# Four key units of linear attention projected at later tiles of the feed-forward, in a fused attention and feed-forward kernel

## The chip, the cores and the metric

The kernel runs on one core of a Trainium2 chip. The metric is the device time of one execution in microseconds (us).

## What is computed

A linear attention over 8 batches of 8 heads, 576 tokens and 64 channels, with 128 projected features that are taken with both signs, and then a feed-forward network on its output (4608 tokens, 512 to 2048 to 512 channels) with the Mish function in the middle. All in float32.

```
def phi(x):
    proj = np.einsum('bhsd,df->bhsf', x, w_phi)
    proj = proj - np.max(np.abs(proj), axis=-1, keepdims=True)
    return np.concatenate([np.exp(proj), np.exp(-proj)], axis=-1)
q_p, k_p = (phi(q), phi(k))
kv = np.einsum('bhsf,bhsd->bhfd', k_p, v)
z = np.sum(k_p, axis=2)
num = np.einsum('bhsf,bhfd->bhsd', q_p, kv)
den = np.einsum('bhsf,bhf->bhs', q_p, z)[..., None] + 1e-06
x = num / den            # heads side by side: 4608 x 512
h = x @ w_in
sp = np.where(h > 20.0, h, np.log1p(np.exp(np.minimum(h, 20.0))))
g = h * np.tanh(sp)
out = g @ w_out
```

## The kernel before

**Work on the keys.** Two heads make a pair, the 32 pairs of all batches lie behind each other, and their 18432 rows are cut into 36 key units of 512 rows, 0 to 35. A unit has five steps. `k_load` fetches its 256 KB; `v_load` fetches the values of the pairs that begin in it (two `v` buffers); `k_proj` multiplies by `w_phi` into two PSUM banks, and DVE takes the maximum of the absolute values (L174) and subtracts it (L175) into two `e` tiles, of which there are six; `k_exp` makes the two exponentials of each tile on ACT (L216, L217), two calls per unit; `k_sum` multiplies with the values into an open sum `kvps` of the pair, which a DVE copy (L233) ends. A pair has 576 rows, so its sum stays open from one unit to the next and keeps one of the four banks of the pool `ps_att`. That pool also serves the projections, the transposes `dt`, the numerators `num` and the sums of the weights' low parts.

**Work on the queries.** The tokens are cut into 18 chunks of 256, each in two groups of heads. `q_proj` projects (for chunks after the first, one of its two banks is from the pool `ps_h`, which has two and serves the feed-forward too), `q_turn` transposes and makes the exponentials (L251, L253), `q_num` multiplies with the sums, `q_out` transposes the result (L278). The numerator of (2, 0), chunk 2 and group 0, needs the sums up to pair 5, and (2, 1) needs those up to pair 7, which ends with key unit 8.

**The feed-forward.** For a chunk it has 16 tiles of 128 hidden channels. `ff_in` makes one tile (twelve matmuls, L300), after every second one `mish` follows (L308, a table of ACT other than that of the exponential), which is split in a high and a low part (L312 on ACT, L313 on DVE), and `ff_out` (L330) follows some four tiles later. Chunks 0 and 1 are worked on in halves: tiles 0 to 7 are the first half of chunk 0, 8 to 15 the first half of chunk 1, 16 to 23 and 24 to 31 the second halves. The partial sums of the first halves are copied away by ACT (L335). Both weights are split into parts in the kernel as well: `split_weight` uses ACT (L118, L119, L131), DVE (L121 to L125) and POOL (L127, L135, L136), 32 times, from tile -13.2 to tile 20.1. Its word tiles share three buffers with the tiles `u` of Mish.

**The order.** Each step is an event with a time, in units of feed-forward tiles, and the program calls the steps in the order of these times (L349 to L397). TensorE works in that order exactly. The other engines' queues are ordered by a planner, which goes by its own costs; only the activations with a table keep the program's order among them (`table`, L151). `FIRST_STEPS` (L35 to L37) lists the first steps by hand, as (time, key unit, query). From tile 14 on a loop adds one key unit and one query group every eight tiles: at 14 key unit 9 with query (2, 0), at 22 key unit 10 with query (2, 1).

A step at time t without a query and after tile 1 sets its other times from its own alone: the loads at t - 4 (`v_load` at t), the projection at t - 0.04, the exponentials at t + 1.2 and t + 1.7, the sum at t + 3.77:

```
if not first and not query:
    exps, tsum = (t + 1.2, t + 1.7), t + 3.8
```

Of the kernel before, what the change touches and what calls it, by code (L numbers as in the profile page):

```python
# [32 lines left out]
NK, LEAD = B * NHP * S // 512, 5  # L33

FIRST_STEPS = ((-14.0, 0, None), (-12.5, 1, None), (-11.0, 2, None), (-9.5, 3, None), (-8.0, 4, None), (-6.6, None, 0),  # L35
               (-5.2, None, 1), (-2.0, None, 2), (1.0, None, 3), (5.0, 5, None), (7.0, 6, None), (9.0, 7, None),
               (11.0, 8, None))  # L37

FE0, FE1, FSUM, FX, FLAST = 0.9, 1.2, 2.1, 3.1, 1.0
E0, E1, GX = 0.27, 0.36, 0.6  # L40
# [389 lines left out]
```

## Time and profile before

| | us |
|---|---|
| median of three runs | 1200.73 |
| lowest and highest of them | 1200.13, 1201.69 |
| the profiled execution | 1200.22 |
| its span, first to last instruction | 1198.40 |
| TensorE busy (matmul) | 1143.7 |
| ACT busy | 639.0 |
| DVE busy | 471.7 |
| POOL busy | 97.6 |

A row of the timeline gives the start, the duration, engine, line, operation, the output and the inputs, and the count of instructions merged in it. In square brackets stands how long the engine was idle just before, and what ended that.

### The profile page before, as it was taken

What the parts mean: (1) busy time and instruction counts of PE and PEld (TensorE: products, weight loads), DVE (VectorE), ACT (ScalarE), POOL (GpSimd) and SP (SyncE); (2) the same over time, 40 slices, a digit from 0 to 9 for tenths busy, and PEclk for the clock granted to TensorE, in tenths of its full rate; (3) what the DMA queues carried; (4) which work ended last, traced back from release to release, by engine and by line L of the source; (5) the groups of instructions that cost most, each with busy time, mean ns of one, the idle gap of its engine ahead of it and who ended that gap; (6) DMA issues with size and microseconds to landing.
All of it is one profiled execution on the core that took longest, in us unless ns stands there. A gap on an engine that the chain in (4) does not pass through costs nothing.

```text
span 1198.4 us, 26666 instructions
## 1 busy us (share of the span) xinstructions
PE 1143.7 (95%) x11696; PEld 1018.5 (85%) x11696; DVE 471.7 (39%) x977; ACT 639.0 (53%) x1051; POOL 97.6 (8%) x86
## 2 busy tenths in 40 slices
PE   6788877999999999999999999999999999999998
PEld 5666766999898989898989898998989898998997
DVE  4655888443333333333333333333333332222311
ACT  6867756555555555555554545454545455555422
POOL 2233667000000000000000000000000000000000
PEclk9899888999999999999999999999999999999999
DMA  9901110111111111101111111001111100000000
GB/s 349 354 27 30 59 29 19 48 48 29 40 31 48 29 38 30 35 25 45 31 48 30 48 31 39 28 30 48 30 48 31 47 19 28 1 19 19 1 19 18
DMA packets 25028, 57.68 MB, mean 48 GB/s; under 512 B 2768, under 2 KB 2896, under 8 KB 24912
## 3 DMA queue, kind: packets, MB, share of 16 engines
q1 hardware_dynamic: 24912, 55.98, 13.8%
q8 instruction: 92, 1.51, 0.5%
q14 instruction: 24, 0.20, 0.1%
HBM read 46.53 MB, written 9.44 MB: 47 GB/s over the span
## 4 chain that ended last, share of the span: by engine, by line
PE 81%; ACT 8%; DVE 4%; DMA 2%; issue 2%; POOL 1%; SPq 0%; ACTq 0%; POOLq 0%; DVEq 0%
PE h L300 32%; PE o L330 29%; PE num L184 6%; PE kvps L184 6%; PE pp_q L169 3%; PE pp_k L169 2%; PE dt L251 2%; DMA words_out<-w_out 2%; ACT L253 1%; ACT e_q L253 1%; PE xt L278 1%; ACT gh L312 1%; ACT e_k L216 1%; ACT e_k L217 1%; DMA kraw<-qT 1%
## 5 line engine op out<-in xcount | busy, mean ns | idle before, releaser
L300 PE MATMUL h<-xTh,win 128*128 128x256 f32 x2304 | 463.9, 285 | 12.2 <-DVE e_q L175 8.0
L300 PEld LDWEIGHTS h<-xTh,win 128*128 128x128 f32 x2304 | 375.8, 190 | 26.5 <-issue 8.4
L330 PE MATMUL o<-wout,gh 128*128 128x512 f32 x1152 | 370.7, 403 | 9.6 <-ACT part L335 5.6
L313 DVE TENSOR_TENSOR gl<-u,gh 128x256 fp32r<-128x256 f32 x288 | 125.9, 456 | 570.3 <-ACT gh L312 562.7
L300 PE MATMUL h<-xTl,win 128*128 128x256 f32 x1152 | 325.9, 283 | 0.0
L330 PEld LDWEIGHTS o<-wout,gh 128*128 128x128 f32 x1152 | 197.8, 189 | 42.9 <-ACT osb L343 9.2
L330 PE MATMUL o<-wout,gl 128*128 128x512 f32 x576 | 228.2, 396 | 0.0
L300 PEld LDWEIGHTS h<-xTl,win 128*128 128x128 f32 x1152 | 218.9, 190 | 8.4
L308 ACT ACTIVATE u<-h 128x512 f32<-128x512 f32 x144 | 86.1, 598 | 173.1 <-PE h L300 165.8
L281 ACT CAST xTh<-xt 128x512 fp32r<-128x512 f32 x36 | 21.2, 589 | 287.7 <-PE xt L278 287.2
L330 PEld LDWEIGHTS o<-wout,gl 128*128 128x128 f32 x576 | 108.7, 189 | 26.6
L312 ACT CAST gh<-u 128x256 fp32r<-128x256 f32 x288 | 110.6, 408 | 18.7 <-PE o L330 6.4
L184 PE MATMUL kvps<-v,e_k 128*64 128x66 f32 x2560 | 88.2, 229 | 6.6 <-ACT e_k L217 6.6
L308 ACT ACT_TABLE_LOAD x73 | 93.7, 1283 | 1.3
L184 PEld LDWEIGHTS kvps<-v,e_k 128*64 128x64 f32 x2560 | 82.5, 143 | 13.7 <-ACT e_k L217 7.5
L253 ACT ACTIVATE e_q<-dt 128x512 f32<-128x512 f32 x144 | 77.9, 596 | 14.4 <-PE dt L251 14.1
L253 ACT ACT_TABLE_LOAD x64 | 82.1, 1283 | 1.0
L184 PE MATMUL num<-kv,e_q 128*64 128x66 f32 x2304 | 74.8, 222 | 1.7 <-DVE e_k L175 1.3
L184 PEld LDWEIGHTS num<-kv,e_q 128*64 128x64 f32 x2304 | 70.9, 137 | 5.4 <-issue 4.6
L169 PEld LDWEIGHTS pp_k<-w_phi,kraw 64*128 64x128 f32 x576 | 38.8, 199 | 25.2 <-issue 21.4
L169 PE MATMUL pp_k<-w_phi,kraw 64*128 64x128 f32 x576 | 46.7, 299 | 12.8 <-issue 5.4
L174 DVE TENSOR_REDUCE m_k<-pp_k 128x4 f32<-128x512 f32 x72 | 46.5, 685 | 22.6 <-PE pp_k L169 22.6
(70 smaller groups left out, 851.4 us busy)
## 6 DMA issues: line engine op xcount, KB each, us to landing
v<-va SPq DMA_DIRECT2D x32, 330.0 KB, 3.4
kraw<-kT SPq DMA_DIRECT2D x36, 256.0 KB, 2.7
out<-osb SPq DMA_DIRECT2D x36, 256.0 KB, 2.0
qraw<-qT SPq DMA_DIRECT2D x35, 256.0 KB, 2.6
words_in<-w_in SPq DMA_DIRECT2D x16, 512.0 KB, 8.7
words_out<-w_out SPq DMA_DIRECT2D x16, 512.0 KB, 8.7
kraw<-qT SPq DMA_DIRECT2D x1, 256.0 KB, 8.6
w_phi<-w_phi SPq DMA_DIRECT2D x1, 64.0 KB, 1.8
```

Source lines behind the costliest of these rows:

```text
L169: nc.tensor.matmul(ps[j][:, n], raw[rows, n * P:(n + 1) * P], w_phi2[rows], start=True, stop=True)
L174: nc.vector.tensor_reduce(m, ps[j], axis=AX.X, op=ALU.max, apply_absolute_value=True)
L184: nc.tensor.matmul(ps[rows], lhsT[:, rows], rhs[h], start=start, stop=stop, skip_group_check=True)
L216: table(nc.scalar.activation(e[:, 1, :], e[:, 0, :], AF.Exp))
L251: nc.tensor.transpose(ps[:, n * P:(n + 1) * P], e[:, 0, n * P:(n + 1) * P], ident)
L253: table(nc.scalar.activation(e[:, s, :], ps, AF.Exp, scale=2.0 * s - 1.0))
L281: nc.scalar.copy(hi, ps)
L300: nc.tensor.matmul(ps, w[:, wcol], x[:, cc % 2, :], start=(n == 0), stop=(n == 11))
L308: table(nc.scalar.activation(u, hv, AF.Mish))
L312: nc.scalar.copy(gh, u[:, f * CH:(f + 1) * CH])
L313: nc.vector.tensor_sub(gl, u[:, f * CH:(f + 1) * CH], gh.bitcast(F32))
L330: nc.tensor.matmul(ps, g[:, cols], w, start=(i == first and k == 0), stop=(i == end and k == 2))
```

## The change

Four times in `FIRST_STEPS` are other ones. Key units 5, 6, 7 and 8 have 5, 7, 9 and 11 before, and 6, 9, 12 and 16 after.

```
 FIRST_STEPS = ((-14.0, 0, None), (-12.5, 1, None), (-11.0, 2, None), (-9.5, 3, None), (-8.0, 4, None), (-6.6, None, 0),
-               (-5.2, None, 1), (-2.0, None, 2), (1.0, None, 3), (5.0, 5, None), (7.0, 6, None), (9.0, 7, None),
-               (11.0, 8, None))
+               (-5.2, None, 1), (-2.0, None, 2), (1.0, None, 3), (6.0, 5, None), (9.0, 6, None), (12.0, 7, None),
+               (16.0, 8, None))
```

All steps of these units move with it, by 1, 2, 3 and 5 tiles. Unit 8 is now projected at 15.96 and summed at 19.77, so its projection comes after that of unit 9 and query (2, 0) at tile 14, and its sum still before that of unit 9 at 21.97. The raw keys of unit 8 are asked for at 12 instead of 7, after those of unit 9 and query (2, 0) at 10. The values of pair 8, asked for at 14, come in the program ahead of the sum of unit 7, which moves from 12.77 to 15.77.

## Rows read from the trace of the kernel before

**Rows 1.** Busy time by stretch, columns in its first line: around the change, and the rest.

```profile
core 0: us, PE busy (x) PEld busy (x) DVE busy (x) ACT busy (x) POOL busy (x), PEclk, DMA share, GB/s
115.00:190.00 75.00, 57.32 (x577) 49.64 (x574) 57.65 (x80) 52.58 (x81) 49.47 (x37) 0.86 0.13 41
260.00:1190.00 930.00, 925.67 (x9405) 834.67 (x9404) 308.81 (x697) 465.54 (x766) 0.00 (x0) 1.00 0.10 31
```

**Rows 2.** TensorE's waits, 90 to 215 us: us in total, times, longest.

```profile
PE h L300 <- DVE e_q L175: 8.0, 1, 8.0
PE o L330 <- ACT part L335: 5.6, 2, 2.9
PE h L300 <- POOL win L136: 4.1, 2, 3.7
PE pp_k L169 <- ACT wout L147: 2.5, 1, 2.5
```

**Rows 3.** Timeline of TensorE, the five places A to E.

```profile
120.28 1.42 PE L169 MATMUL pp_k<-w_phi,kraw 64*128 64x128 f32 x14 [2.50 <-ACT wout L147]
...
141.22 1.00 PE L330 MATMUL o<-wout,gh 128*128 128x512 f32 x2 [2.88 <-ACT part L335]
...
159.85 0.55 PE L300 MATMUL h<-xTh,win 128*128 128x256 f32 x1 [8.04 <-DVE e_q L175]
...
187.20 0.79 PE L300 MATMUL h<-xTh,win 128*128 128x256 f32 x2 [3.72 <-POOL win L136]
...
193.22 1.22 PE L330 MATMUL o<-wout,gh 128*128 128x512 f32 x2 [2.73 <-ACT part L335]
```

**Rows 4.** Busy time by stretch, columns as in the first group: behind place C.

```profile
159.00:165.00 6.00, 5.15 (x18) 4.38 (x18) 5.80 (x10) 4.44 (x7) 4.05 (x5) 0.50 0.00 0
```

**Rows 5.** The chain that ended last, in order of time: start, us, what.

```profile
105.92 0.63 ACT e_k L216
...
144.39 0.63 ACT e_k L216
...
147.22 0.68 ACT w_out L118
...
159.10 0.61 DVE e_q L175
```

**Rows 6.** Timeline of TensorE, and groups by line and shape.

```profile
149.15 1.16 PE L169 MATMUL pp_k<-w_phi,kraw 64*128 64x128 f32 x16
165.23 2.15 PE L184 MATMUL kvps<-v,e_k 128*64 128x66 f32 x64
L174 DVE TENSOR_REDUCE m_k<-pp_k 128x4 f32<-128x512 f32 x72 | 46.5, 685 | 22.6 <-PE pp_k L169 22.6
L175 DVE TENSOR_TENSOR e_k<-pp_k,m_k 128x512 f32<-128x512 f32 x72 | 46.7, 681 | 0.0
L216 ACT ACTIVATE e_k<-e_k 128x512 f32<-128x512 f32 x72 | 45.4, 631 | 0.0
```

**Rows 7.** Timeline of DVE, key unit 8 and a weight.

```profile
137.06 1.27 DVE L174 TENSOR_REDUCE m_k<-pp_k 128x4 f32<-128x512 f32 x2
138.25 0.41 DVE L125 TENSOR_SCALAR t_in<-w_in 128x512 uint32<-128x512 uint32 x1
```

**Rows 8.** Timelines of ACT and DVE between C and D.

```profile
169.12 0.62 ACT L131 CAST win<-w_in 128x512 fp32r<-128x512 f32 x1 [4.25 <-POOL t_in L127]
...
180.54 0.60 ACT L308 ACTIVATE u<-h 128x512 f32<-128x512 f32 x1
...
183.33 0.62 ACT L131 CAST win<-w_in 128x512 fp32r<-128x512 f32 x1 [0.87 <-POOL t_in L127]
183.97 1.28 ACT L118 ACT_TABLE_LOAD   x1
...
187.18 0.68 ACT L118 ACTIVATE w_out<-words_out 128x512 f32<-128x512 f32 x1 [0.79 <-POOL win L136]
170.37 1.50 DVE L125 TENSOR_SCALAR t_in<-w_in 128x512 uint32<-128x512 uint32 x1 [2.46 <-POOL wout L136]
```

## The prediction

> **What bounds the kernel now.** I read the page's slices first, then the busy time by stretch. TensorE is the bound after 260 us: there it is busy for 925.67 of 930 us, so nothing there can be won by moving four projections [rows 1]. The first 260 us hold its idle time, and the change lies in 95 to 200 us of them. Between 115 and 190 us TensorE has 57.32 busy us of 75; no other engine fills that stretch either: ACT 52.58, DVE 57.65, POOL 49.47. So this stage is bound by a chain that hops between engines, each of which works through its own queue in order.
>
> The view of TensorE's waits between 90 and 215 us says where that chain ends: the four largest causes come to 20.2 us [rows 2]. I place them by the timeline. A: 2.50 us at 120.28, the projection of key unit 7, for a buffer of `ps_att`. B: 2.88 us at 141.22. C: 8.04 us at 159.85, ff_in of tile 14, which needs the `h` bank that q_proj(2, 0) took and DVE has not read out. D: 3.72 us at 187.20 and the rest of 4.1 behind it, ff_in of tile 20, for the POOL half of splitting the weights `in_*_3`. E: 2.73 us at 193.22 [rows 3]. After the gap C the granted clock stands at 0.50, the lower of the two levels (1.2 of 2.4 GHz), from 159 to 165 us [rows 4]. A gap thus costs more than its length.
>
> The chain of waits, in order of time, shows what C hangs on: from 105.92 us until C ends it runs over ACT, POOL and DVE, and not over TensorE. Key units stand in it by name: an exponential of unit 5 at 105.92, one of unit 8 at 144.39, and, right before C ends, the DVE work of query (2, 0) at 159.10, behind that of unit 9 [rows 5]. A and B don't stand in that chain: taking A or B alone away would only lengthen C. So what counts is how much ACT and DVE have to do ahead of 159.85, and then ahead of 187.
>
> **The change, part by part.** No instruction is added or removed. One key unit is 16 matmuls of 64x128 in a burst of 1.16 us, 64 or 80 sum matmuls (2.15 us in the row at 165.23, where it is 64), two maxima and two subtractions on DVE (2 x 685 + 2 x 681 ns = 2.73 us) and four exponentials on ACT (two pairs of L216 and L217, which write the same shape, so 4 x 631 ns = 2.52 us) [rows 6]. In the chain's rows they count less, since they overlap: two maxima take 1.27 us together, and L125 of a weight, which the chain waits for, starts 1.19 us behind the first of them [rows 7].
>
> ACT first. Mish activations follow each other every second tile, and the exponentials of a unit fall between two of them. Before: unit 5 behind the Mish of tile 5, unit 6 behind 7, unit 7 behind 9, unit 8 behind 11, none behind 13 and 17. After, from exps at t+1.2 and t+1.7: unit 5 behind 7, unit 6 behind 9, none behind 5 and 11, unit 7 behind 13, unit 8 behind 17. So two slots ahead of C (behind 5 and 11) lose their exponentials. Each slot is worth between 0.63 us (the one that stands in the chain) and 2.52 us (all four in series). I take 1.6, the middle, since in 144.39 to 147.22 other casts lie between them: 3.2 us for both.
>
> DVE ahead of C: four key units become three (unit 8 now comes after query (2, 0)). Worth from 0 to 2.73 us; I take 1.2, the delay of L125 that the rows show. Sum ahead of C: 3.2 + 1.2 = 4.4 us, bounds 0 and 7.8.
>
> Table loads: the splits' own activations (L118) pay a load of 1.28 us when they follow a Mish, as behind the Mish of tile 17, at 183.97 [rows 8]. Splits fall into slots 5, 11, 13 and 17 before and after, so I count no load saved and none added. The Trainium skill (ScalarE: Activation LUTs, Table sets: the hidden batching unit) says that cheap functions such as abs stand in every set; by that no load would be due for L118, two would be saved ahead of C and two added after it, which again leaves the sum where it is. Here the timeline does have a load in front of L118, so the row decides.
>
> What comes back after C. Unit 7's exponentials fall behind the Mish of tile 13, where ACT then waits 4.25 us for POOL (169.12): cost 0, bound 2.52 if they are queued ahead of the casts that wait ends with. Unit 8's DVE work lands behind its projection at tile 16, near 168 us, where DVE idles 2.46 us (before 170.37): I take 1.0, for what doesn't fit or pushes L125, bounds 0 and 2.73. Unit 8's exponentials fall behind the Mish of tile 17 (180.54), where ACT has 0.87 and 0.79 us idle: 2.52 - 1.66 = 0.9, bounds 0 and 2.52. TensorE gets the projection (1.16) and the sum (2.15) of unit 8 between C and D instead of ahead of C: 3.3 us, covered by the 4.1 us that it waits at D; uncovered they cost 3.3 [rows 8]. Sum after C: 1.9 us.
>
> Buffers and queues. `ps_att` has four banks, one of them held from k_sum(5) to k_sum(8) by an open `kvps`; the hold now ends at 19.77 instead of 14.77, with q_turn(2, 0) at 16.16 inside it. Its transposes come behind unit 8's two banks and two `kvps`, so the copy of `kvps_6` (L233) must be out: a wait of up to some 2 us ahead of D, under the same cover as the 3.3 us (together 5.3 against 4.1). Six `e` tiles: unit 8 takes unit 7's, free since k_sum(7) was issued just ahead. On SP the raw keys are asked for four tiles early as before. The v of batch 2's first pair (v_load(9), at 14) needs the buffer that k_sum(7) frees, now at 15.77, and SP waits for it; behind it stand only the loads at 18, and the data is wanted at 21.97, six tiles later: nothing.
>
> Sum: -4.4 + 1.9 = -2.5 us on the profiled execution. Its own time is 1200.22 us, 1.82 above its span, and 0.51 below the median of the runs shown (1200.73). The forecast is 1197.7 us.
>
> **The rivals.** What a measurement of this kernel can tell from no change is about 0.2%, here 2.4 us.
>
> (1) The weights set the time. TensorE gets through tile 20 when the split of `in_3_3` is done on POOL, behind 188 us, whatever it gained before. If the relief at slots 5 and 11 is eaten by POOL and ACT waiting for each other (L127, L131, L136), C may end earlier and D grow by as much. For it: D is a wait for POOL, and POOL's queue holds three operations for each weight. Against it: that chain begins at L118 on ACT, which starts earlier with fewer exponentials ahead. Time: 1200.2 +- 2, no change.
>
> (2) Slower: unit 8 becomes the late thing. k_sum(8) at 19.77 stands in TensorE's queue ahead of ff_in 20, and it wants exponentials that stand behind the Mish of tile 17. From the rows: 180.54 + 0.60 (Mish) + 1.28 (table) + 2.52 (exponentials) + 1.2 (two casts between, of 0.62 like the one at 183.33) = 186.2, then 2.15 of sum: tile 20 would begin at 188.4 and not only go on, as now, at 187.20. The cast of `in_3_3` at 183.33 and the copies that E waits for (L335) are pushed by up to 2.5 us each. With both, 2.5 + 2.5 = 5 us: 1205.2. It decides if unit 8's last exponential ends after 187.20 - 2.15 = 185, less what the first half of tile 20 takes. Against it: C comes earlier and carries all of this with it.
>
> (3) More is won: slots and DVE pay in full (7.8 us), and the clock stays at full level at A. Then 1192.4 us or a little less, since C's shorter gap also leaves less at half clock.
>
> **How the numbers follow.** The forecast with (3): 0.46 (its own range 1191 to 1198.3). Rival 1: 0.29. Rival 2: 0.25. For the range I take the lower bound 1191 (7.8 us and somewhat over 1 us of the half clock) and the upper 1206.5 (rival 2 and a further 1.3 for a transpose that waits uncovered: 5.3 - 4.1). This leaves some 2 in 10 outside, as the order of ACT, DVE and POOL is the planner's, and it may change more than these rows show. Faster by over 0.2%: 0.46; within: 0.29; slower: 0.25.
>
> **What would show it.** Right: no exponential of a key unit between the Mish of tile 5 and tile 7; unit 7's projection without the wait A; C's wait ends before 157 us; unit 8's DVE work in an idle stretch near 170 us; D no longer than before. Wrong: TensorE waiting at k_sum(8) for L217; the wait for POOL at tile 20 longer by what C lost; a new wait at the transposes (L251) for DVE; the same 20 us in the view of waits with other names. After 230 us nothing should differ but the offset.

## The result, and the profile after

The changed kernel is slower: 1207.62 us (median of 4 runs, 1206.69 to 1207.91) against 1200.84 for the kernel before, a ratio of 1.0049 with a 95% interval of 1.0037 to 1.0061 (the ratios in this text are those on record for the single runs; the quotient of the two medians is 1.0056, and lies in the interval). The forecast was 1197.7, in a range from 1191 to 1206.5. The profiled execution took 1207.58 us, its span is 1205.8, so 7.4 us more than before.

TensorE's waits between 90 and 215 us in the changed kernel (us in total, times, longest; it answers to [rows 2]):

```profile
PE h L300 <- ACT u L308: 9.3, 1, 9.3
PE num L184 <- DVE e_k L175: 6.0, 1, 6.0
PE kvps L184 <- ACT e_k L217: 3.6, 3, 1.7
PE pp_k L169 <- DVE e_k L175: 3.2, 1, 3.2
PE dt L251 <- DVE kv L233: 1.7, 1, 1.7
PE lo_out L144 <- ACT wout L147: 1.7, 1, 1.7
```

Of the four causes of [rows 2] the first has another releaser and the other three are gone: no wait for a bank at unit 7 (A), for POOL at tile 20 (D), or for the copies L335 (B, E). In their place stand others. A's releaser L147 is there again, at a weight's low-part sum (L144), and unit 9's projection waits 3.2 us for a bank. The largest new one is 6.0 us at the numerators `num`.

A sum of waits doesn't say which of them cost the time. For that I follow one and the same instruction in both timelines and see where the distance grows. TensorE before, then after, around tile 22 (key unit 10's projection, the second bank of the numerators, the projection of query (2, 1), the transposes of q_out(2, 0)):

```profile
198.23 1.16 PE L169 MATMUL pp_k<-w_phi,kraw 64*128 64x128 f32 x16
...
203.70 1.16 PE L184 MATMUL num<-kv,e_q 128*64 128x66 f32 x32 [1.34 <-DVE e_k L175]
204.79 1.16 PE L169 MATMUL pp_q<-w_phi,qraw 64*128 64x128 f32 x16
...
208.80 0.82 PE L278 MATMUL xt<-ident,x 128*128 128x128 f32 x4
```

```profile
198.64 1.16 PE L169 MATMUL pp_k<-w_phi,kraw 64*128 64x128 f32 x16
...
208.73 2.03 PE L184 MATMUL num<-kv,e_q 128*64 128x66 f32 x32 [5.97 <-DVE e_k L175]
210.69 2.08 PE L169 MATMUL pp_q<-w_phi,qraw 64*128 64x128 f32 x16
...
216.36 0.60 PE L278 MATMUL xt<-ident,x 128*128 128x128 f32 x4
```

Up to unit 10's projection the changed kernel is 0.41 us late. At the second numerator it is 5.03 late, since the wait there is 5.97 instead of 1.34, and at the transposes 7.56, since TensorE then works at the lower clock: the same numerators take 2.03 us instead of 1.16, the projection 2.08 instead of 1.16. The stretch behind the wait, in the changed kernel (columns as in [rows 1]), has a granted clock of 0.50, the lower level:

```profile
208.00:213.00 5.00, 4.27 (x49) 3.95 (x50) 2.82 (x9) 0.59 (x1) 3.67 (x3) 0.50 0.01 3
```

So nearly the whole loss, 7.2 of 7.4 us, lies in one place, at a step that the diff doesn't name. The second numerator needs a bank of `ps_att`; four are out (two of unit 10's projection, the open `kvps`, the first numerator), and the first to come back is the one that DVE's subtraction of unit 10 (L175) empties. DVE's timeline says why that is late. Before:

```profile
200.87 0.43 DVE L125 TENSOR_SCALAR t_out<-w_out 128x512 uint32<-128x512 uint32 x1
201.21 1.28 DVE L174 TENSOR_REDUCE m_k<-pp_k 128x4 f32<-128x512 f32 x2
202.41 0.55 DVE L121 TENSOR_SCALAR w_out<-w_out 128x512 f32<-128x512 f32 x1
202.87 1.27 DVE L175 TENSOR_TENSOR e_k<-pp_k,m_k 128x512 f32<-128x512 f32 x2
```

After:

```profile
201.79 0.43 DVE L125 TENSOR_SCALAR t_out<-w_out 128x512 uint32<-128x512 uint32 x1
202.13 0.42 DVE L121 TENSOR_SCALAR w_out<-w_out 128x512 f32<-128x512 f32 x1
202.59 1.40 DVE L122 TENSOR_SCALAR w_out<-w_out 128x512 uint32<-128x512 uint32 x1
204.02 0.69 DVE L123 SCALAR_TENSOR_TENSOR w_out<-words_out,w_out 128x512 uint32<-128x512 uint32 x1
204.63 1.48 DVE L313 TENSOR_TENSOR gl<-u,gh 128x256 fp32r<-128x256 f32 x1
206.04 0.41 DVE L125 TENSOR_SCALAR t_out<-w_out 128x512 uint32<-128x512 uint32 x1
206.38 0.41 DVE L313 TENSOR_TENSOR gl<-u,gh 128x256 fp32r<-128x256 f32 x1
206.71 1.28 DVE L174 TENSOR_REDUCE m_k<-pp_k 128x4 f32<-128x512 f32 x2
```

Both queues come to the end of weight 30 (L125) within 0.92 us of each other. Before, unit 10's maxima are next. After, the four steps of weight 31 and the low part of the Mish of tile 21 have been put ahead of them, 4.6 us of work, while TensorE has had unit 10's projection ready since 199.8. DVE is 0.92 us late; the rest of the wait is other work that stands first.

### The profile page after: what moved, and what is told of

It is laid out like the page before. It is cut to its first block, busy times and chain, and to the rows that moved or that the text cites. A ratio compares the mean times of both kernels' runs of the same rounds, so it can differ in the third digit from the quotient of the medians.

```text
span 1205.8 us, 26671 instructions
## 1 busy us (share of the span) xinstructions
PE 1145.4 (95%) x11696; PEld 1020.8 (85%) x11696; DVE 470.1 (39%) x977; ACT 638.1 (53%) x1051; POOL 97.5 (8%) x86
## 4 chain that ended last, share of the span: by engine, by line
PE 80%; ACT 9%; DVE 4%; DMA 2%; issue 2%; POOL 1%; SPq 1%; ACTq 0%; POOLq 0%; DVEq 0%
PE h L300 31%; PE o L330 28%; PE num L184 6%; PE kvps L184 5%; PE pp_q L169 3%; PE pp_k L169 2%; PE dt L251 2%; DMA words_out<-w_out 2%; ACT L253 1%; ACT e_q L253 1%; PE xt L278 1%; ACT e_k L217 1%; ACT e_k L216 1%; ACT gh L312 1%; DMA kraw<-qT 1%
## 5 line engine op out<-in xcount | busy, mean ns | idle before, releaser
L313 DVE TENSOR_TENSOR gl<-u,gh 128x256 fp32r<-128x256 f32 x288 | 122.1, 443 | 567.1 <-ACT gh L312 559.2
L184 PE MATMUL kvps<-v,e_k 128*64 128x66 f32 x2560 | 89.3, 231 | 10.2 <-ACT e_k L217 10.1
L184 PEld LDWEIGHTS kvps<-v,e_k 128*64 128x64 f32 x2560 | 83.3, 144 | 17.2 <-ACT e_k L217 12.1
L184 PE MATMUL num<-kv,e_q 128*64 128x66 f32 x2304 | 75.6, 223 | 6.4 <-DVE e_k L175 6.0
L184 PEld LDWEIGHTS num<-kv,e_q 128*64 128x64 f32 x2304 | 71.7, 138 | 10.1 <-issue 9.4
```

Source lines behind the costliest of these rows:

```text
L184: nc.tensor.matmul(ps[rows], lhsT[:, rows], rhs[h], start=start, stop=stop, skip_group_check=True)
L313: nc.vector.tensor_sub(gl, u[:, f * CH:(f + 1) * CH], gh.bitcast(F32))
```

## The experiments

Two theories stood against each other. The DVE-order theory is the one above. The late-unit-8 theory is rival 2 of the prediction: TensorE does wait at k_sum(8) for the exponentials L217, 1.18 and 1.65 us, and this could be carried to the end (in the chain that ended last, unit 8's exponentials stand from 184.08 to 187.95 us, ahead of weight 30 on DVE):

```profile
185.89 0.45 PE L184 MATMUL kvps<-v,e_k 128*64 128x66 f32 x8 [1.18 <-ACT e_k L217]
188.00 3.35 PE L184 MATMUL kvps<-v,e_k 128*64 128x66 f32 x56 [1.65 <-ACT e_k L217]
```

Each run was timed beside the kernel before on the same chip; ratios are to that.

**1. Changed kernel, unit 10 a tile earlier.**

```
-            at(t - 0.04, k_proj, key)
+            at(t - (0.04 if key != 10 else 1.04), k_proj, key)
```

> The changed kernel, with the projection of key unit 10 one tile earlier in TensorE's order (20.96 instead of 21.96), so that DVE's queue has its maxima behind weight 30 again, as before the change, and not behind weight 31 and the Mish of tile 21. DVE-order theory: the wait of q_num(2,0) for L175 falls from 6.0 us to under 2, no half clock follows, and the time is 1200 to 1202.5. Late-unit-8 theory (TensorE's 2.8 us at k_sum(8) for L217, carried on): nothing of that is touched, the time stays at 1205 to 1208.

1201.67 us against 1201.8, ratio 0.9996 (0.9988 to 1.0005): the whole loss is gone. On DVE the maxima stand behind weight 30, and the wait is 1.64 us; the waits for L217 are as they were. TensorE and DVE in this run:

```profile
188.45 3.13 PE L184 MATMUL kvps<-v,e_k 128*64 128x66 f32 x56 [1.66 <-ACT e_k L217]
...
205.07 1.16 PE L184 MATMUL num<-kv,e_q 128*64 128x66 f32 x32 [1.64 <-DVE e_k L175]
```

```profile
202.24 0.43 DVE L125 TENSOR_SCALAR t_out<-w_out 128x512 uint32<-128x512 uint32 x1
202.58 1.28 DVE L174 TENSOR_REDUCE m_k<-pp_k 128x4 f32<-128x512 f32 x2
```

The late-unit-8 theory, which expected 1205 to 1208, falls.

**2. Changed kernel, unit 10 behind the numerators.** The same line with 0.015 instead of 1.04.

> The changed kernel, with the projection of key unit 10 behind q_num(2,0) in TensorE's order instead of ahead of it, so that the numerators find free PSUM banks; DVE's queue still has weight 31 and the Mish of tile 21 ahead of unit 10's maxima. If the wait for a bank at the numerators is the loss: that wait is gone; what TensorE now waits for is the projection's bank, for the short DVE work on the numerators, 1 to 3 us; 1201 to 1204. Late-unit-8 theory: 1205 to 1208.

1205.83 us, ratio 1.0039 (1.0025 to 1.0052), outside what I expected. The numerators wait no longer, but unit 10's projection does, 4.60 us for L268 of the numerators, which stands behind the same weight 31 and the same Mish on DVE:

```profile
207.57 1.83 PE L169 MATMUL pp_k<-w_phi,kraw 64*128 64x128 f32 x13 [4.60 <-DVE r L268]
```

So it isn't the place of the bank in TensorE's order. Whoever comes to DVE at this point waits; I had thought that short work on DVE would also be started soon.

**3. Kernel before, with DVE's order as after.** Ahead of the maxima of unit 10 (in the code, `red` is the maximum):

```
+            if name == "k_10":
+                for first in ("out_15_0", "0_6"):
+                    tc.add_manual_dep(red.ins, behind[first].name, ...)
```

(`behind` keeps the last DVE step, L125, of each weight and the last low part, L313, of each Mish.)

> The kernel before, with one thing of the changed one: on DVE the first maximum of key unit 10 is held behind the last step of weight 31 (L125) and behind the low part of the Mish of tile 21, by an order on DVE's own queue. DVE-order theory: the numerators wait 5 to 7 us instead of 1.3, with half clock behind it, and the time is 1205 to 1208. Late-unit-8 theory: unit 8 is early here, so nothing is lost but the longer wait partly: 1201 to 1203.

1207.87 us, ratio 1.0056 (1.0043 to 1.0068), with all four key units where they were before:

```profile
206.86 1.27 DVE L175 TENSOR_REDUCE m_k<-pp_k 128x4 f32<-128x512 f32 x2
...
208.73 0.67 DVE L180 TENSOR_TENSOR e_k<-pp_k,m_k 128x512 f32<-128x512 f32 x1
```

```profile
208.88 1.72 PE L189 MATMUL num<-kv,e_q 128*64 128x66 f32 x32 [4.66 <-DVE r L273]
```

The line names L273 as releaser, a short step between the two subtractions. The wait of 4.66 us is a little under the 5 to 7 expected. Not all of this run's time is the forced order's: in its profile unit 10's projection is already 1.87 us late (200.10 against 198.23; the waits for L335 and for POOL are 6.9 and 5.2 us in total there, where [rows 2] have 5.6 and 4.1). It isn't the chip, for run 4, taken on the same one, has 5.6 and 3.9. The transposes of q_out(2, 0) are 6.71 us late (215.51 against 208.80). So 6.71 - 1.87 = 4.84 of the 6.4 us by which its span of 1204.8 us is longer arise at tile 22, from the forced order.

**4. Control: kernel before, unit 10 a tile earlier.**

> The control of the first: the kernel before with the projection of key unit 10 one tile earlier. Its numerators wait only 1.3 us, so by the DVE-order theory there is at most that and a little clock to win: 1198.5 to 1201.5. If moving unit 10 is a gain by itself (then the first run would say nothing of the change): under 1197.

1200.3 us, ratio 0.9992 (0.9983 to 1.0000): as expected, and not a gain that these runs can tell from none. So the 6 us that the same edit gives back in run 1 are the change's own.

**5. The forecast's relief, taken outright.** Units 5 and 8, in the kernel before:

```
+        if n in (5, 8):
+            table(nc.scalar.activation(e[:, 0, :P], e[:, 0, :P], AF.Exp, scale=-1.0))
+            return
...
-                        halves(ps[:, j, s], es[j][:, s, i * P:(i + 1) * P], (vt...
+                        halves(ps[:, j, s], es[j][:, 0, :P] if n in (5, 8) else es[j][:, s, i * P:(i + 1) * P], (vt...
```

and for unit 8 maximum and subtraction over one block of 128 columns of four. The kernel leaves out most of these units' exponentials, so its output is not the reference's.

> The kernel before with most of what the forecast counted as relief taken away outright, to size it. Key units 5 and 8 make only one exponential of 128 columns per tile instead of two of 512, unit 8 also only a quarter of its maxima and subtractions; their sums read that slice instead, so TensorE's instructions stay and the output is not the reference's. By the forecast's steps (1.6 us for a slot with all exponentials, 1.2 us for the DVE work of a unit, here some 0.8 of each): C ends 3 us earlier, near 157, and the time falls by 3 us. If the weights set the time (rival 1): C ends earlier, the wait for POOL at tile 20 grows by the same, and the time moves by less than 1 us.

1199.27 us, ratio 0.9979 (0.9971 to 0.9988). The total, 2.5 us, is near the 3 us expected, but it doesn't come the way that was forecast: C ends at 160.19, not earlier than before, and D is longer:

```profile
160.19 0.58 PE L304 MATMUL h<-xTh,win 128*128 128x256 f32 x1 [7.16 <-ACT u L312]
...
187.91 0.79 PE L304 MATMUL h<-xTh,win 128*128 128x256 f32 x2 [4.87 <-POOL win L136]
```

What is gained comes with the copies L335, waits for which fall from 5.6 us to 2.8: E is gone, what is left is at B, and unit 10's projection starts at 196.12 instead of 198.23. With less work ahead C does not move. The Mish that it now waits for stands on ACT behind the splits' casts (L131), which wait for POOL, and waits for POOL itself:

```profile
155.43 0.62 ACT L131 CAST wout<-w_out 128x512 fp32r<-128x512 f32 x1 [3.01 <-POOL t_out L127]
156.06 1.28 ACT L312 ACT_TABLE_LOAD   x1
159.54 0.60 ACT L312 ACTIVATE u<-h 128x512 f32<-128x512 f32 x1 [2.19 <-POOL wout L136]
```

**6. Run 1, with the sum of unit 8 behind tile 20.** `at(tsum - 0.03 if key != 8 else 20.6, k_sum, key)`.

> The first experiment (changed kernel, key unit 10 projected a tile earlier), and also the sum of key unit 8 behind ff_out of tile 20 (20.6 instead of 19.77), so that TensorE doesn't wait for the exponentials L217 ahead of tile 20. If that wait of 2.8 us is what ate the forecast's gain: 1.5 to 3 us less than the first experiment, 1198.5 to 1200.5. If the split weights set when tile 20 ends anyway (rival 1): tile 20 waits for POOL instead, and the time is that of the first experiment, within 1 us.

1204.2 us, ratio 1.0020 (1.0011 to 1.0028); both expectations missed. Tile 20 does wait for POOL instead (2.26 us), and then the ff_out behind it, that of tile 16, for the copies L335 (4.18 us):

```profile
190.38 0.38 PE L300 MATMUL h<-xTh,win 128*128 128x256 f32 x1 [2.26 <-POOL win L136]
...
195.65 1.22 PE L330 MATMUL o<-wout,gh 128*128 128x512 f32 x2 [4.18 <-ACT part L335]
197.22 3.79 PE L184 MATMUL kvps<-v,e_k 128*64 128x66 f32 x64
```

The sum, now behind these gaps, runs at the lower clock (granted 0.50 from 197 to 201 us; it takes 3.79 us, where [rows 6] have 2.15). At 19.77 the sum covers the time that TensorE waits for POOL here.

**7. Unit 8 at tile 13 instead of 16.** `(6.0, 9.0, 12.0, 13.0)`.

> The changed kernel with key unit 8 at tile 13 instead of 16, units 5 to 7 as changed, nothing else. DVE's queue then has unit 10's maxima behind weight 30 and the first step of weight 31, as before the change. DVE-order theory: the numerators wait 1 to 2 us and the time is 1199.5 to 1203. If spreading units 5 to 7 were itself the loss: 1205 or more.

1202.37 us, ratio 1.0005 (0.9996 to 1.0014). The numerators don't wait at all. Units 5 to 7 in their new places, with unit 8 at 13, cost nothing that can be told.

**8. Unit 8 alone.** `(5.0, 7.0, 9.0, 16.0)`.

> Unit 8 alone moved: tiles 5, 7, 9 and 16. On DVE the maxima of unit 10 then come behind three steps of weight 31, and its subtractions behind the Mish of tile 21. DVE-order theory: the numerators wait 5 to 6 us for L175, 1205 to 1208, nearly the whole loss of the change. If the four moves share the loss: about 1202 to 1204.

1205.71 us, ratio 1.0029 (1.0018 to 1.0039). It is slow, but the wait at the numerators is 2.98 us and not 5 to 6; C is longer than before (11.13 us against the 8.04 of [rows 3]). Unit 10's projection is 2.65 us late (200.88), the transposes 5.82 (214.62): of the 5.5 us by which its span is longer, some 3.2 arise at tile 22 and the rest ahead of it.

```profile
162.47 0.55 PE L300 MATMUL h<-xTh,win 128*128 128x256 f32 x1 [11.13 <-DVE e_q L175]
...
207.98 1.16 PE L184 MATMUL num<-kv,e_q 128*64 128x66 f32 x32 [2.98 <-DVE e_k L175]
```

**9. Changed kernel, weight 31 split later.** `WTIMES[31] = 23.1`. TensorE's order stays as changed.

> The changed kernel with the split of weight 31 at 23.1 instead of 20.125, nothing else. It has no step on TensorE, so TensorE's order stays as changed. On DVE its four steps (some 2.9 us) then come behind unit 10's maxima; the Mish of tile 21 (some 1.9 us) still stands ahead of them. DVE-order theory: a part of the loss comes back, in proportion: the numerators wait 2.5 to 4.5 us instead of 6.0, and the time is 1203 to 1206. Late-unit-8 theory: no change, 1206.5 to 1208.5.

1204.24 us, ratio 1.0021 (1.0012 to 1.0030). With weight 31 out of the way and the Mish of tile 21 still ahead, the wait is 3.17 us:

```profile
207.94 1.16 PE L185 MATMUL num<-kv,e_q 128*64 128x66 f32 x32 [3.17 <-DVE e_k L176]
```

This is a dose in the middle. But not all of this run's loss is at tile 22: unit 10's projection is already 2.41 us late (200.64), the transposes 4.24 (213.04), so 1.83 of the 4.0 us by which its span is longer arise there, just what the wait has more than the 1.34 before. The ratios are thus no clean measure of the dose (2.41 us were lost elsewhere here, 2.65 in run 8, 1.87 in run 3). A cleaner one is the time from the start of k_sum(9) to the transposes of q_out(2, 0) on TensorE, which holds the numerators:

| | wait at the numerators, us | k_sum(9) to the transposes, us | ratio |
|---|---|---|---|
| run 4 | none | 7.91 | 0.9992 |
| run 7 | none | 8.39 | 1.0005 |
| kernel before | 1.34 | 9.48 | 1 |
| run 1 | 1.64 | 9.77 | 0.9996 |
| run 8 | 2.98 | 12.64 | 1.0029 |
| run 9 | 3.17 | 11.30 | 1.0021 |
| run 3 | 4.66 | 14.32 | 1.0056 |
| the change | 5.97 | 16.63 | 1.0049 |

Run 8 is out of line with run 9 because the clock falls behind its wait: the projection of query (2, 1) takes 1.83 us there and 1.16 in run 9.

**10. POOL's share of in_\*_3 taken out.** In the kernel of run 4, the four splits without L135 and L136; the low part is the rest alone:

```
+            if not (kind == "in" and j == 3):
                 nc.gpsimd.tensor_sub(wf, wf, hi.bitcast(F32))
                 nc.gpsimd.tensor_tensor(lo, wf, rest, op=ALU.add)
+            else:
+                nc.vector.tensor_copy(lo, rest)
```

> The kernel before with unit 10 projected a tile earlier (as in the fourth experiment), and the four splits of in_*_3 without POOL's last two steps: the low part is the rest alone, copied by DVE, so the output is less exact. POOL then has 8 operations of 1.3 to 1.4 us less ahead of tile 20. If the weights set when tile 20 goes on: the wait for POOL (4 us) is gone, and with the clock behind it the time falls by 3 to 7 us against the fourth experiment, 1194 to 1198. If key units and ACT's queue set it: tile 20 waits for something else, and the time moves by less than 1.5 us.

1201.99 us, ratio 1.0005 (0.9996 to 1.0013). POOL is gone from TensorE's waits, and nothing is won:

```profile
PE o L333 <- ACT part L338: 9.9, 4, 5.2
PE h L303 <- DVE e_q L178: 7.7, 1, 7.7
PE pp_k L172 <- ACT wout L150: 2.5, 1, 2.5
PE h L303 <- ACT win L131: 2.3, 1, 2.3
```

The copies L335 (here L338) wait longer on ACT, and tile 20 waits for a cast of ACT (L131). Rival 1 had tile 20 go on when POOL is done with its split; with POOL out of the way, TensorE waits for ACT's queue instead.

**11 and 12. Two tries for a faster kernel**, both on run 4: the splits of in_\*_3 earlier and those of out_8 to out_11 later (`(11.5, 14.5), (12.5, 15.5)` in WTIMES), and `NSUMMED` 18 instead of 16 (two more weights without L135 and L136 on POOL; their L121 goes from DVE to POOL, so POOL loses two operations and not the four that I counted, and the two it gets are short, 0.6 us).

> A try for a faster kernel, from the same finding: the fourth experiment with the splits of in_*_3 a tile or so earlier (12.5 to 15.5 instead of 13.5 to 17) and those of out_8 to out_11 a tile later (11.5 to 14.5). If POOL's order allows it, tile 20's wait of 4 us shrinks by 2 or 3 us: 1197 to 1200. If the buffers that splits and Mish share hold it up: 1200 to 1204.

> A second try: the fourth experiment with 18 instead of 16 weights whose low part TensorE sums, so POOL loses four operations ahead of tile 16 and TensorE gets six or so matmuls more, with two more PSUM banks passing through. If POOL's queue is what delays the later splits, the chain moves ahead by 2 to 4 us and the time falls to 1196 to 1199.5. If not, TensorE's own extra work and waits for banks show: 1200 to 1204.

1204.75 us (1.0031, 1.0019 to 1.0042) and 1201.38 us (0.9999, 0.9990 to 1.0007): neither is faster. In the first the wait for POOL is gone, but 11.1 us of waits for Mish stand there, and the waits for L335 have grown from 5.6 to 9.0; in the second TensorE waits 5.4 us for POOL. No run with the reference's whole work beats the kernel before by more than the runs can tell.

## Why the prediction was wrong, point by point

**The step that failed is the sum: it left out a term, and the relief ahead of C in it was too large.** It ran from C to D and took what follows tile 20 as given: "So what counts is how much ACT and DVE have to do ahead of 159.85, and then ahead of 187." It had no term for the numerators at tile 22. The cause was in the view of waits that I read, as `num L184 <- DVE e_k L175`, 1.34 us; I kept the four largest and dropped it. It measured 5.97, and with the clock behind it the loss is 7.16 of the 7.4 us: 4.63 of wait, and 2.53 between the second numerator and the transposes (208.80 - 203.70 = 5.10 before, 216.36 - 208.73 = 7.63 after). Run 1 takes this loss away, run 3 makes most of it in the kernel before, and run 9 gives it in part. The second failure is smaller: the relief of 4.4 us ahead of C came to 1.25, and so even with the loss at tile 22 taken away nothing is left of the 2.5 us (run 1: 0.9996, interval 0.9988 to 1.0005).

**What was said of queues.** The text went through `ps_att` at tile 16, the `e` tiles and SP, and what it found there held (the wait at the transposes L251 for the copy L233 is 1.69 us, where it had up to 2, and no wait of TensorE's ends with a load on SP). It had no wait for a bank at unit 9's projection, where 3.17 us stand, nor at the numerators. And it treated the order on DVE as that of the rows before, and said only in the range that it may change. It did change, at an instruction that the diff doesn't touch.

**Ahead of C: 4.4 us.** C ended at 158.60, 1.25 us earlier, and by a Mish on ACT instead of DVE. Unit 5's slot was empty, as said, unit 7 no longer waited at A, and the table loads came out as counted (16 between 100 and 195 us before, 16 after; in the emptied slots the load stands in front of L118, at 107.95 and 141.15). The count for the other case, that L118 needs none, was off: a slot without exponentials then saves the load for them and that for the next Mish, so four ahead of C against four behind it, and the sum stays the same. But run 5 cut the exponentials in the same two slots down to short ones, and C didn't move; the slots of 1.6 us were not in series with C. The rows that put single exponentials in the chain were true, yet without them the chain went through the neighbours: POOL's steps of the splits and the casts that wait for them. In the changed kernel:

```profile
145.50 1.83 PE L169 MATMUL pp_k<-w_phi,kraw 64*128 64x128 f32 x13 [3.17 <-DVE e_k L175]
...
158.60 0.58 PE L300 MATMUL h<-xTh,win 128*128 128x256 f32 x1 [9.34 <-ACT u L308]
```

```profile
156.02 0.62 ACT L131 CAST wout<-w_out 128x512 fp32r<-128x512 f32 x1 [2.21 <-POOL t_out L127]
156.66 1.28 ACT L308 ACT_TABLE_LOAD   x1
157.95 0.60 ACT L308 ACTIVATE u<-h 128x512 f32<-128x512 f32 x1
```

Unit 9's projection at 145.50 shows the mechanism of tile 22 once more: it waits for the subtraction of unit 7, whose maxima DVE begins at 139.04, 6.6 us after that projection's end (132.41), behind steps of weights, one of which waits 2.40 us for POOL. Here TensorE waits for C afterwards anyway; whether this delay moved C was not tried.

**After C: 1.9 us.** Unit 8's DVE work did not fall into the idle stretch near 170: its first maximum is at 178.20, 9.2 us behind the start of the projection (168.96), between the steps of the last in_\*_3 weights. Its last exponential ends near 188, beyond the 185 that rival 2 named, and TensorE waits 2.83 us at k_sum(8). Rival 2's mechanism was thus there, but not its price: D and E were gone, and unit 10's projection is 0.41 us late. That its 1205.2 lies nearest to the measured time is luck: the loss comes from tile 22, which it doesn't name. Without the loss at tile 22 the change is worth nothing that these runs can tell (run 1: 0.9996; its median is 1.4 us above that of run 4, the kernel before with the same edit, and their intervals overlap), where the forecast had -2.5 us.

**Rival 1** was nearest for the tiles up to 20: what C gained was not to be had later. But D did not grow by it, it was gone, and run 10 says that POOL alone isn't it.

**The signs.** Of the four signs of being wrong three came: the wait at k_sum(8) for L217, the one at the transposes for DVE, and the waits under other names (28.4 us in all between 90 and 215 us, where the kernel before has 22.9). The fourth, a longer wait for POOL, did not. None of them names the numerators.

**What stays open.** Why the planner put weight 31 and the Mish ahead of unit 10 in the one kernel and not in the other was not tried. Nor was what makes runs 3 and 9 lose a further 1.87 and 2.41 us ahead of tile 22, so that run 3 with 4.66 us of wait is as slow as the change with 5.97. Why run 8 has a longer C, with units 5 to 7 where they were, is open too.

## What to carry to other kernels

Where one engine's order is written by hand and the others' by a planner, a moved step changes queues that the diff doesn't mention: compare each engine's order before and after, and look first for instructions that free a buffer and now have other work ahead of them. Price every short wait in the region and behind it, not only the largest ones: a wait of 1.3 us that hangs on a queue's order can become 6, and a wait of 8 us may not move at all. To find where a loss lies, follow the same instruction through both timelines; the place where the distance jumps is where to look for the cause, and an order forced onto the kernel before can show it.

## What the runs showed of the hardware

The clock behind a gap in TensorE's work is not the same each time. Behind the 5.97 us of the change the granted clock is 0.50, the lower level, for 5 us. Behind the 3.17 us of run 9 it stays at the full level, while behind the 2.98 us at the same place in run 8 it is 0.66 from 208 to 213 us, and behind the 2.50 us of A in the kernel before it is 0.59 in 122 to 125 us, means of both levels, so the length of a gap alone doesn't tell (run 9, then the kernel before):

```profile
208.00:213.00 5.00, 5.00 (x66) 4.53 (x67) 4.31 (x11) 0.00 (x0) 1.06 (x1) 1.00 0.21 52
```

```profile
122.00:125.00 3.00, 3.00 (x15) 2.92 (x15) 2.21 (x4) 2.67 (x5) 1.76 (x2) 0.59 0.25 87
```
